# A gated mix of two linear-attention blocks: the second block's x^T phi(k) in seven half-size products, and the query sums of the output stage in quarters

## The chip, the cores and the metric

The kernel runs on one core of one Trainium2 chip. The metric is device time in microseconds (us), less is better. TensorE (PE in the profile) multiplies matrices, with its weight loads shown apart as PEld; VectorE is DVE, ScalarE is ACT, GpSimd is POOL, and SyncE (SP) issues DMAs. Matrix products land in PSUM, eight banks of 128 x 512 fp32; everything else lives in SBUF.

## What is computed

```python
def block(x, wqkv, wo):                  # x 2048 x 640, H = 32 heads of 20
    q, k, v = split_heads(x @ wqkv)
    phi = lambda t: where(t > 0, t + 1, exp(t)) + 1e-6
    pq, pk = phi(q), phi(k)
    kv = einsum("bhsd,bhse->bhde", pk, v)
    z = einsum("bhsd->bhd", pk)
    num = einsum("bhqd,bhde->bhqe", pq, kv)
    den = einsum("bhqd,bhd->bhq", pq, z)[..., None] + 1e-6
    return merge_heads(num / den) @ wo
g = sigmoid((x * gate_w).sum(-1, keepdims=True))
out = g * block(x, A_wqkv, A_wo) + (1 - g) * block(x, B_wqkv, B_wo)
```

All inputs and the output are bf16. Both blocks, A and B, take the same x.

## The kernel before

S = 2048 rows of x lie in 16 tiles of 128 (`xn`, rows on partitions) and transposed in 5 tiles of 128 columns (`xT`). For each block the kernel goes through these steps:

- **K pass** (`k_chunk`, L214): 16 chunks of x times Wk in PSUM; `phi` (L193) makes phi(k) of them: an exponential on ACT (L196), a clamp (L199) and a maximum (L203) on DVE. The result is `pk`.
- **Q pass** (`q_pass`, L601): ten units of x times Wq, transposed, through the same `phi`, into `pqT`. Between units stand the column sums z (`z_rows`, `z_pass`).
- **G stage** (`g_all`, L621): GT = x^T phi(k), a 640 x 640 matrix, so that V need not be formed. In between run the denominators (`rec_pass`, L432: products, then on DVE a scaling at L441 and a reciprocal at L446) and five calls of `norm_unit` (L482), each of which spreads the reciprocals with eight matmuls into two PSUM slots and multiplies a fifth of `pqT` by them. The gate is folded into these factors. In block A each slot is first copied to SBUF by ACT (L501) and multiplied on DVE at L503; in block B only the second slot is (`if jj == 1 or b == 0`), and the first is read by DVE from PSUM.
- **KVT and M**: `kvt_pass` (L392) makes Wv^T GT, of which DVE keeps the head-diagonal blocks (L409); `m_unit` (L416) multiplies by Wo. M is 640 x 640 for each block.
- **Output stage**: out = pqA M_A + pqB M_B, by seven half-size products instead of eight (Strassen's scheme in Winograd's form). `Pair` i makes output tiles i and i + 8; p1 to p7 are its products of five matmuls each, `out_add` (L518) the sums on DVE. The scheme needs three row sums of the queries, `p_sums` (L458): k = 1 into `pqT[0]`, k = 2 and 4 into `xT`; a difference `p_diff` into `D3`; and sums of M, `m_sums`, into `TM`.

**G in block A and in block B.** Block A computes the fifth column tile of GT directly (`g_pass`, L273: 16 row tiles x 2 halves = 32 matmuls of 320 columns) and the other four by seven products (`g_strassen`, L315; `g_prod`, L306, is one product of 16 matmuls). That form needs four sums of x, `x_sum` (L289, kept in `SX`), and four of phi(k), `k_sum` (L299, kept in `TK`, which borrows block B's `pqT`). `SX` borrows `D3`, `M[0]` and `M[1]`. Block B computes all five column tiles directly: four `g_pass` calls and `g_last` (L356).

**What sets the order.** Each engine works through its instructions in the order in which they were issued; inside `with tc.manual_schedule()` that is the order of the code, outside it a scheduler decides. Before, `g_all(1, zsel)` (L688) stands outside. PSUM slots are given out in rotation (`ps`, L63): a matmul that starts a slot waits until DVE or ACT has read what was in it. The output stage opens its own banks after `banks.close()`.

The three sums `p_sums(slice(0, HB))` (L698) for the rows of pairs 0 to 3 come first in the output stage, and one sum each for the rows of pairs 4 to 7 after pairs 1, 2 and 3:

```python
            if i < 4:
                p_sums(slice(HB, SH), ((1,), (2,), (4,))[i - 1])
```

Of the kernel before, what the change touches and what calls it, by code (L numbers as in the profile page):

```python
# [8 lines left out]
P = 128  # L9
# [21 lines left out]
def kernel(  # L31
# [31 lines left out]
    def ps(name, slot=None):  # L63
# [17 lines left out]
    grow = persist.tile([1, D], BF16, name="grow")  # L81
    D3 = persist.tile([P, DT, SH], BF16, name="D3")
    d3_flat = D3[:].rearrange("p c s -> p (c s)")
    m_flat = [t[:].rearrange("p c d -> p (c d)") for t in M]
    hc, ic = ST // 2, 2 * P
    SX = {k: t[:, o:o + hc * ic].rearrange("p (i c) -> p i c", i=hc)
          for k, t, o in ((1, d3_flat, 0), (2, d3_flat, hc * ic), (3, m_flat[0], 0), (4, m_flat[1], 0))}
    t_flat = pqT[1][:].rearrange("p c s -> p (c s)")
    TK = {k: t_flat[:, n * hc * HF:(n + 1) * hc * HF].rearrange("p (i d) -> p i d", i=hc)
          for n, k in enumerate((1, 2, 3, 4))}  # L90
    lift = persist.tile([P, 1], FP32, name="lift")
    TM = [None] * 4
# [29 lines left out]
    nc.sync.dma_start(out=wq[0][:], in_=wq_dram[0][:, :, 0:D])  # L122
    nc.gpsimd.dma_start(out=grow[:], in_=gate_w.rearrange("(o f) -> o f", o=1))
# [97 lines left out]
    def k_first():  # L221

        pts = [ps("kA", (2 + i) % 4) for i in (0, 1)]

        def part(i, cs):
            for c in cs:
                for hf in range(2):
                    k_mm(0, i, c, pts[i], hf)

        for i in range(2):  # L230
            x_transpose(i, i, "dve", (0, 2, DT))
        for i in range(2):
            part(i, (0, 1))
        x_transpose(2, 0, "dve")
        for i in range(2):
            part(i, (2,))
        pts.append(ps("kA", 1))
        part(2, (0, 1, 2))
        x_transpose(3, 0, "act")
        for i in range(3):  # L240
            part(i, (3, 4))
            k_done(0, i, pts[i])
        k_chunk(0, 3, 0)
# [55 lines left out]
    def k_sum(k):  # L299
# [3 lines left out]
        a, b = {1: (b12, b11), 2: (b22, TK[1]), 3: (b22, b12), 4: (b21, TK[2])}[k]  # L303
        add_rows(TK[k], a, b, ALU.subtract)
# [10 lines left out]
    def g_strassen(norm):  # L315

        x11, x12 = [xn[:, k:k + hc, 0:ic] for k in (0, hc)]
        x22 = xn[:, hc:ST, ic:2 * ic]
        b11 = pk[:, 0:hc, 0:HF]
        b21, b22 = [pk[:, hc:ST, n * HF:(n + 1) * HF] for n in range(2)]  # L320
        lo, hi = slice(0, HF), slice(HF, D)

        def temp(name):
            return work.tile([P, 2, HF], FP32, tag="gt", name=name, bufs=3)

        def add(dst, pt, sb):
            nc.vector.tensor_tensor(out=dst, in0=pt[:, :, 0:HF], in1=sb[:], op=ALU.add)

        even, odd = ps("gs0", 0), ps("gs1", 1)
        g_prod(even, x11, b11, True)  # L330
        p1 = temp("p1")
        nc.scalar.copy(out=p1[:], in_=even[:, :, 0:HF])
        g_prod(odd, SX[2], TK[2], True)
        u2 = temp("u2")
        add(u2[:], odd, p1)
        k_sum(4)
        norm()
        g_prod(even, x12, b21, False)
        nc.scalar.copy(out=GT[:, 0:2, lo], in_=even[:, :, 0:HF])
        norm()  # L340
        x_sum(4)
        g_prod(odd, SX[3], TK[3], False)
        u3 = temp("u3")
        add(u3[:], odd, p1)
        norm()
        even = ps("gs0", 0)
        g_prod(even, SX[1], TK[1], True)
        add(GT[:, 2:4, hi], even, u3)
        norm()
        g_prod(odd, x22, TK[4], False)  # L350
        add(GT[:, 2:4, lo], odd, p1)
        g_prod(even, SX[4], b22, False)
        add(GT[:, 0:2, hi], even, u2)
        norm()

    def g_last(b, c, slots):  # L356

        for hf, slot in enumerate(slots):
            pt = ps(f"g{'AB'[b]}", slot)
            for i in range(ST):  # L360
                g_mm(c, i, hf, pt)
            nc.scalar.copy(out=GT[:, c, hf * HF:(hf + 1) * HF], in_=pt[:, hf, 0:HF])
# [119 lines left out]
    def norm_unit(b, parts, rts, slots):  # L482

        pts = [ps(f"ex{'AB'[b]}", s) for s in slots]
        for k, (m, h) in enumerate(parts):
            for j in range(4):
                nc.tensor.matmul(  # L487
                    pts[j // 2][:, j % 2, k * RB:(k + 1) * RB], lhsT=E4[32 * j:32 * j + 32, m * P:(m + 1) * P],
                    rhs=rts[h][32 * j:32 * j + 32, :], start=True, stop=True,
                )  # L490
        (m0, h0), (m1, h1) = parts
        for jj in range(2):
            src = pts[jj][:].rearrange("p j (k n) -> p j k n", n=RB)
            if h0 == h1:
                r0 = h0 * 2 * HB + jj * HB
                dst = pqT[b][:, m0:m1 + 1, r0:r0 + HB].rearrange("p k (j n) -> p j k n", n=RB)
            else:
                dst = pqT[b][:, m0, :].rearrange("p (k u j n) -> p u j k n", k=2, u=2, n=RB)[:, jj]
            if jj == 1 or b == 0:
                ex = work.tile([P, 2, 2, RB], BF16, tag="ex", name="ex")  # L500
                nc.scalar.copy(out=ex[:], in_=src)  # L501
                src = ex[:]
            nc.vector.tensor_tensor(out=dst, in0=src, in1=dst, op=ALU.mult)  # L503
# [17 lines left out]
    def tmp(name):  # L521
        return work.tile([P, HF], FP32, tag=name, name=name)

    class Pair:

        def __init__(self, i):
            self.i = i
            self.osb = [work.tile([P, D], BF16, tag=f"osb{k}", name=f"osb{k}", bufs=3) for k in range(2)]
# [9 lines left out]
        def p2(self):  # L538
            prod(self.at("w"), pqT[1][:, :, 0:SH], M[1][:, :, 0:HF], self.i, True)
            out_add(self.osb[0][:, 0:HF], self.at("w"), self.p1s[:])  # L540
# [4 lines left out]
        def p6(self):  # L545
            prod(self.at("x"), xT[:, :, 0:SH], TM[1], self.i, False)
            self.u2 = tmp("u2")
            nc.scalar.copy(out=self.u2[:], in_=self.at("x"))  # L548
            self.u3 = tmp("u3")
# [17 lines left out]
        def p4(self):  # L567
            prod(self.at("y"), pqT[1][:, :, SH:S], TM[3], self.i, False)
            out_add(self.osb[1][:, 0:HF], self.at("y"), self.u2[:])
            nc.sync.dma_start(out=rows_of(self.i + ST // 2), in_=self.osb[1][:])  # L570
# [24 lines left out]
    def tm_pair(tag, ks):  # L595

        t = wpool.tile([P, 2, DT, HF], BF16, tag=tag, name="TM" + tag)
        for n, k in enumerate(ks):
            TM[k] = t[:, n]

    def q_pass(b, units):  # L601
# [11 lines left out]
        for k, (m, h) in enumerate(units):  # L613
            if b == 1 and k == 3:
                turn[0] = (turn[0] + 1) % 4
            if b == 0 and k < 2:
                (k_sum, x_sum)[k](2 + k)
            q_unit(b, m, h, b == 0)
        return zsel

    def g_all(b, zsel):  # L621

        units = [((m, h), (m + 1, h)) for h in range(2) for m in (0, 2)] + [((DT - 1, 0), (DT - 1, 1))]

        def norm():
            norm_unit(b, units.pop(0), rts, (2, 3))
# [37 lines left out]
    wk[1] = load_w(1, "k", nc.sync)  # L664
    with tc.manual_schedule():
        gate_columns()
        k_chunk(0, ST - 1)
        k_sum(1)
# [14 lines left out]
        load_wo(1, nc.sync)  # L683
        zsel = q_pass(1, [(m, h) for h in range(2) for m in range(DT)])
        tm_pair("wk", (0, 3))
        add_rows(TM[0], M[0][:, :, HF:D], M[0][:, :, 0:HF], ALU.subtract)
    tm_pair("wq", (1, 2))
    g_all(1, zsel)  # L688
    def late_pool(name):
        return tc.tile_pool(name=name, bufs=1, space=bass.MemoryType.PSUM, reuse_waits="tile")  # L690

    def bank(pool, name, n=1):
        return pool.tile([P, HB] if n == 1 else [P, n, HB], FP32, tag=name, name=name)

    banks.close()
    outer = ctx.enter_context(late_pool("outer"))
    with tc.manual_schedule():
        p_sums(slice(0, HB))  # L698
        half = ST // 2
        acc = {k: [bank(outer, f"o{k}{n}") for n in range(2)] for k in "xz"}  # L700
# [79 lines left out]
```

## Time and profile before

| | us |
|---|---|
| median of three runs (198.02 to 198.65) | 198.16 |
| the profiled execution | 197.97 |
| its span, first to last instruction | 196.2 |
| PE busy | 191.6 |
| DVE busy | 148.8 |
| ACT busy | 82.3 |

A line of a view gives the engine, the line of the kernel, the operation, what it writes and reads ("out<-in"), how often, and how long. In the chain of waits each line is a start, a length and the work on the path that ended last. In the timeline it is start, length, engine, line, operation, and in brackets the idle time before it and what ended that. The 1.8 us that the profiled execution's time has over its span lie before the first and behind the last instruction; the output's DMAs end there.

### The profile page before, as it was taken

The page shows a single profiled execution, that of the slowest core. Times are in us where ns is not written, and L with a number is a line of the kernel's source. Part 1 is how long each engine was busy: PE and PEld are TensorE (multiplying, and loading weights), DVE is VectorE, ACT ScalarE, POOL GpSimd, SP SyncE. Part 2 cuts the span into 40 slices and gives each one's busy share as a digit, 9 for nine tenths or more (in the row PEclk, how much of TensorE's full clock was granted, in tenths as well). Part 3 has the DMA queues.
Part 4 walks back from the last instruction along what each step waited for, and adds up shares of the span by engine and source line. Part 5 has one row for each costly group of instructions (what it writes and reads, how often), then busy time and mean ns, then how long its engine had stood idle before and what let it go on. Part 6 is the DMA issues. An engine that isn't in the chain of part 4 may idle for free.

```text
span 196.2 us, 3675 instructions
## 1 busy us (share of the span) xinstructions
PE 191.6 (98%) x1520; PEld 122.8 (63%) x1520; DVE 148.8 (76%) x242; ACT 82.3 (42%) x110; POOL 9.2 (5%) x23
## 2 busy tenths in 40 slices
PE   8999999999999999999999999999999999999992
PEld 3656557664576666777764444576667777777771
DVE  4288868898989896888887677768779798885553
ACT  2155455555931874366652554413552520122110
POOL 7920000000000000000000000000000000000000
PEclk9999999999999999999999999999999999999999
DMA  6976569970050000320071000000000002122112
GB/s 188 306 148 72 104 161 373 252 196 6 2 167 3 0 0 3 78 89 3 0 158 36 2 0 0 0 3 0 3 0 0 3 0 100 72 82 78 72 70 69
DMA packets 18318, 14.22 MB, mean 72 GB/s; under 512 B 8782, under 2 KB 18302, under 8 KB 18302
## 3 DMA queue, kind: packets, MB, share of 16 engines
q1 hardware_dynamic: 17694, 13.34, 25.6%
q10 hardware_dynamic: 576, 0.66, 0.9%
q8 instruction: 12, 0.20, 0.4%
q14 instruction: 4, 0.03, 0.0%
q0 software_dynamic: 32, 0.00, 0.0%
HBM read 9.40 MB, written 2.62 MB: 61 GB/s over the span
## 4 chain that ended last, share of the span: by engine, by line
PE 95%; DVE 2%; ACT 1%; issue 0%; DVEq 0%; ACTq 0%
PE gB L284 11%; PE kB L206 11%; PE qB L251 11%; PE kA L206 10%; PE gs L310 8%; PE qA L251 7%; PE ox L514 6%; PE oy L514 5%; PE oz L514 5%; PE qA L262 4%; PE ow L514 2%; PE gA L284 2%; PE warm L154 2%; PE mA L427 1%; DVE osb L519 1%; PE xt L187 1%
## 5 line engine op out<-in xcount | busy, mean ns | idle before, releaser
L206 PEld LDWEIGHTS <-xT 128*128 128x128 bf16 x320 | 31.1, 99 | 13.1 <-DVE xT L191 0.4
L199 DVE TENSOR_SCALAR e<-e 128x640 bf16<-128x640 bf16 (+1 forms) x52 | 19.3, 371 | 12.4 <-ACT e L196 11.5
L284 PEld LDWEIGHTS <-xn 128*128 128x128 bf16 x192 | 18.3, 98 | 8.4 <-issue 1.3
L206 PE MATMUL kA<-wkA,xT 128*128 128x320 bf16 x160 | 23.5, 304 | 0.0
L284 PE MATMUL gB<-pk,xn 128*128 128x320 bf16 x160 | 22.9, 299 | 0.0
L206 PE MATMUL kB<-wkB,xT 128*128 128x320 bf16 x160 | 22.9, 299 | 0.0
L251 PE MATMUL qB<-xT,wqB 128*128 128x512 bf16 x100 | 22.0, 379 | 0.0
L251 PEld LDWEIGHTS <-wqB 128*128 128x128 bf16 x100 | 9.6, 98 | 11.4 <-issue 0.3
L196 ACT ACTIVATE e<-kB 128x640 bf16<-128x640 f32 x16 | 11.3, 705 | 10.7 <-PE kB L206 10.7
L196 ACT ACTIVATE e<-qB 128x1024 bf16<-128x1024 f32 x10 | 10.2, 1024 | 13.1 <-PE qB L251 13.1
L203 DVE SCALAR_TENSOR_TENSOR pk<-kA,e 128x640 bf16<-128x640 f32 x16 | 13.2, 824 | 2.0 <-PE kA L206 0.5
L196 ACT ACTIVATE e<-qA 128x1024 bf16<-128x1024 f32 x10 | 10.2, 1024 | 10.7 <-PE qA L262 5.3
L196 ACT ACTIVATE e<-kA 128x640 bf16<-128x640 f32 x16 | 11.1, 706 | 8.2 <-PE kA L206 7.5
L203 DVE SCALAR_TENSOR_TENSOR pk<-kB,e 128x640 bf16<-128x640 f32 x16 | 13.2, 824 | 1.7
L251 PE MATMUL qA<-xT,wqA 128*128 128x512 bf16 x60 | 13.6, 379 | 0.0
L203 DVE SCALAR_TENSOR_TENSOR pqTB<-qB,e 128x1024 bf16<-128x1024 f32 x10 | 12.2, 1224 | 1.4 <-DVE e L199 0.5
L548 ACT COPY u<-ox 128x320 f32<-128x320 f32 x8 | 3.4, 428 | 20.9 <-PE ox L514 20.9
L501 ACT CAST ex<-exA 128x1024 bf16<-128x1024 f32 x10 | 9.6, 1017 | 5.8 <-PE exA L487 4.9
L514 PEld LDWEIGHTS <-xT 128*128 128x128 bf16 x85 | 8.1, 98 | 2.9
L251 PEld LDWEIGHTS <-wqA 128*128 128x128 bf16 x60 | 5.7, 98 | 6.7 <-issue 0.3
L514 PEld LDWEIGHTS <-pqTA 128*128 128x128 bf16 x85 | 8.0, 98 | 2.9
L514 PEld LDWEIGHTS <-pqTB 128*128 128x128 bf16 x80 | 7.8, 98 | 3.0
(118 smaller groups left out, 272.7 us busy)
## 6 DMA issues: line engine op xcount, KB each, us to landing
out_dram<-osb SPq DMA_DIRECT2D x15, 160.0 KB, 1.8
xn<-in_A_x_dram SPq DMA_DIRECT2D x3, 640.0 KB, 6.2
wqA<-in_A_wqkv_dram SPq DMA_DIRECT2D x1, 800.0 KB, 6.0
wvA<-in_A_wqkv_dram SPq DMA_DIRECT2D x1, 800.0 KB, 10.2
wkB<-in_B_wqkv_dram SPq DMA_DIRECT2D x1, 800.0 KB, 5.2
wqB<-in_B_wqkv_dram SPq DMA_DIRECT2D x1, 800.0 KB, 4.8
wvB<-in_B_wqkv_dram SPq DMA_DIRECT2D x1, 800.0 KB, 4.7
woA<-in_A_wo_dram SPq DMA_DIRECT2D x1, 750.0 KB, 13.7
```

Source lines behind the costliest of these rows:

```text
L154: nc.tensor.matmul(warm[:, 0, :], lhsT=one_l, rhs=one_r, start=True, stop=True)
L196: nc.scalar.activation(out=e[:], in_=src, func=ACT.Exp)
L199: nc.vector.tensor_scalar(e[:], e[:], 1.0, EPS, op0=ALU.min, op1=ALU.add)
L203: nc.vector.scalar_tensor_tensor(out=dst, in0=src, scalar=1.0 + EPS, in1=e[:], op0=ALU.add, op1=ALU.max)
L206: nc.tensor.matmul(pt[:, hf, 0:HF], lhsT=xT[:, c, i * P:(i + 1) * P], rhs=wk[b][:, c, hf * HF:(hf + 1) * HF], start=(c == 0), stop=(c == D ...
L251: nc.tensor.matmul(pt[:, u, :], lhsT=wq[b][:, c, m * P:(m + 1) * P], rhs=xT[:, c, n * HB:(n + 1) * HB], start=(c == 0), stop=(c == DT - 1),)
L262: nc.tensor.matmul(pt[:, u, :], lhsT=wq[b][:, c, (m + u) * P:(m + u + 1) * P], rhs=xT[:, c, n * HB:(n + 1) * HB], start=(c == 0), stop=(c ...
L284: nc.tensor.matmul(pt[:, hf, 0:HF], lhsT=xn[:, i, c * P:(c + 1) * P], rhs=pk[:, i, hf * HF:(hf + 1) * HF], start=(i == 0), stop=(i == ST - 1),
L310: nc.tensor.matmul(pt[:, n, 0:HF], lhsT=left[:, i, n * P:(n + 1) * P], rhs=right[:, i, :], start=(first and i == 0), stop=(i == hc - 1), s ...
L501: nc.scalar.copy(out=ex[:], in_=src)
L514: nc.tensor.matmul(dst, lhsT=left[:, c, r0:r0 + P], rhs=right[:, c, :], start=(first and c == 0), stop=(c == DT - 1), skip_group_check=not ...
L548: nc.scalar.copy(out=self.u2[:], in_=self.at("x"))
```

## The change

- **Block B's GT by `g_strassen`.** `g_all` has one form for both blocks: `g_pass` for the fifth column tile, a `k_sum`, `rec_pass`, `g_strassen`. `g_last` goes. The sums of x of block A are kept: `S3` is a tensor of its own for SX 1 to 3 (before they lay in `D3` and `M[0]`), SX 4 stays in `M[1]`, which block B fills only afterwards. Block B's sums of phi(k) go into `xT` and, the first, into the slot of `wkB`; two of them are made in the Q pass or at its end, one before `rec_pass`, one in `g_strassen`. The difference `TM[0]` moves from behind the Q pass into it.
- **Order within `g_strassen`.** In block B the fifth `norm` stands ahead of the seventh product, in block A behind it.
- **`norm_unit`** copies both slots by ACT in both blocks.
- **`g_all(1, zsel)`** and what follows are inside the hand-written order.
- **`p_sums` in quarters** of 256 rows: the first quarter's three sums behind the last G sum, behind `kvt_pass` and behind the two first p2; the second quarter's three within the turn of pair 1; the third and fourth two at a time after pairs 2 to 4. The sum that was at the end of `p2` is a step of its own, `c11`, and comes later for pairs 0 and 1.
- **Room.** `grow` shares the slot of `zr`, the temporaries of `Pair` those of `ex` and `zr`, the two output halves of a pair lie in one tile that shares a slot with p1, u2 and u3 of `g_strassen`. The output stage's banks are taken in the order z, x instead of x, z.
- **At the start** the fourth transpose of x is copied out of PSUM by DVE instead of ACT.

```diff
-        x_transpose(3, 0, "act")
+        x_transpose(3, 0, "dve")
...
-        g_prod(odd, SX[2], TK[2], True)
+        g_prod(odd, SX[2], TK[b][2], True)
         u2 = temp("u2")
         add(u2[:], odd, p1)
-        k_sum(4)
+        k_sum(b, 4)
         norm()
         g_prod(even, x12, b21, False)
         nc.scalar.copy(out=GT[:, 0:2, lo], in_=even[:, :, 0:HF])
         norm()
-        x_sum(4)
-        g_prod(odd, SX[3], TK[3], False)
+        if b == 0:
+            x_sum(4)
+        g_prod(odd, SX[3], TK[b][3], False)
...
-        g_prod(odd, x22, TK[4], False)
+        g_prod(odd, x22, TK[b][4], False)
         add(GT[:, 2:4, lo], odd, p1)
+        if b == 1:
+            norm()
         g_prod(even, SX[4], b22, False)
         add(GT[:, 0:2, hi], even, u2)
-        norm()
+        if b == 0:
+            norm()
...
-            if jj == 1 or b == 0:
-                ex = work.tile([P, 2, 2, RB], BF16, tag="ex", name="ex")
-                nc.scalar.copy(out=ex[:], in_=src)
-                src = ex[:]
-            nc.vector.tensor_tensor(out=dst, in0=src, in1=dst, op=ALU.mult)
+            ex = work.tile([P, 2, 2, RB], BF16, tag="ex", name="ex")
+            nc.scalar.copy(out=ex[:], in_=src)
+            nc.vector.tensor_tensor(out=dst, in0=ex[:], in1=dst, op=ALU.mult)
...
             q_unit(b, m, h, b == 0)
+            if b == 1 and k == 1:
+                k_sum(1, 1)
+            if b == 1 and k == 4:
+                add_rows(TM[0][:], M[0][:, :, HF:D], M[0][:, :, 0:HF], ALU.subtract)
+        if b == 1:
+            k_sum(1, 2)
         return zsel
...
-        if b == 0:
-            g_pass(b, DT - 1, 1)
-            k_sum(3)
-            rts = rec_pass(b, zsel, 2)
-            g_strassen(norm)
-            assert not units
-            return
-        g_pass(b, 0, 1)
+        g_pass(b, DT - 1, 1)
+        k_sum(b, 3)
         rts = rec_pass(b, zsel, 2)
-        g_pass(b, 1, 0)
-        for c in range(2, DT):
-            norm()
-            if b == 1 and c == DT - 1:
-                g_last(b, c, (1, 0))
-            else:
-                g_pass(b, c, (c + 1) % 2, norm if c < DT - 1 else None)
+        g_strassen(b, lambda: norm_unit(b, units.pop(0), rts, (2, 3)))
...
-        p_sums(slice(0, HB))
+        p_sums(part[0], (1,))
...
             pairs[0].p1()
             kvt_pass(1, bank(mid, "mid0", 2))
+            p_sums(part[0], (2,))
             pairs[1].p1()
...
         for p in pairs[0:2]:
             p.p2()
+        p_sums(part[0], (4,))
         m_sums((2, 3, 4), (3,))
         for p in pairs[0:2]:
             p.p7()
             p.p6()
             p.c22()
+            p.c11()
         pairs[0].p4()
         pairs[0].p3()
+        later = {2: (2, (1, 2)), 3: (2, (4,)), 4: (3, (2, 4))}
         for i in range(1, half):
...
             if after is not None:
                 after.p1()
-            if i + 2 < half:
-                after.p2()
-            elif after is None:
-                p.p2()
+            if i == 1:
+                p_sums(part[1], (1,))
+            q = after if i + 2 < half else p if after is None else None
+            if q is not None:
+                q.p2()
+                q.c11()
+            if i == 1:
+                p_sums(part[1], (2,))
             p.p4()
             p.p3(after is None)
-            if i < 4:
-                p_sums(slice(HB, SH), ((1,), (2,), (4,))[i - 1])
+            if i == 1:
+                p_sums(part[1], (4,))
+            if i in later:
+                p_sums(part[later[i][0]], later[i][1])
+            if i == 3:
+                p_sums(part[3], (1,))
```

More of the change, by code (lines that the diff above doesn't have):

```diff
@@ L80, with flat @@
     gwr = persist.tile([P, DT, H], BF16, name="gwr")
-    grow = persist.tile([1, D], BF16, name="grow")
     D3 = persist.tile([P, DT, SH], BF16, name="D3")
-    d3_flat = D3[:].rearrange("p c s -> p (c s)")
-    m_flat = [t[:].rearrange("p c d -> p (c d)") for t in M]
     hc, ic = ST // 2, 2 * P
[L86 to L90, printed above, removed]
+    def flat(t, pattern, inner, at=0):
+        n = hc * inner
+        return t[:].rearrange(pattern)[:, at * n:(at + 1) * n].rearrange("p (i n) -> p i n", i=hc)
+    S3 = persist.tile([P, 3, hc, ic], BF16, name="S3")
+    SX = {k: S3[:, k - 1] for k in (1, 2, 3)}
+    SX[4] = flat(M[1], "p c d -> p (c d)", ic)
+    TK = [{k: flat(pqT[1], "p c s -> p (c s)", HF, k - 1) for k in (1, 2, 3, 4)},
+          {k: flat(xT, "p c s -> p (c s)", HF, k - 2) for k in (2, 3, 4)}]
     lift = persist.tile([P, 1], FP32, name="lift")
-    TM = [None] * 4
+    TM = [persist.tile([P, DT, HF], BF16, name="TM0")] + [None] * 3
     ge = [persist.tile([P, 2 * RB], FP32, name=f"ge{b}") for b in "AB"]
@@ L122 @@
     nc.sync.dma_start(out=wq[0][:], in_=wq_dram[0][:, :, 0:D])
+    grow = work.tile([1, D], BF16, tag="zr", name="grow")
     nc.gpsimd.dma_start(out=grow[:], in_=gate_w.rearrange("(o f) -> o f", o=1))
@@ L297, in x_sum, with k_sum @@
         add_rows(SX[k], a, b, op)
-    def k_sum(k):
+    def k_sum(b, k):
         b11, b12 = [pk[:, 0:hc, n * HF:(n + 1) * HF] for n in range(2)]
         b21, b22 = [pk[:, hc:ST, n * HF:(n + 1) * HF] for n in range(2)]
-        a, b = {1: (b12, b11), 2: (b22, TK[1]), 3: (b22, b12), 4: (b21, TK[2])}[k]
-        add_rows(TK[k], a, b, ALU.subtract)
+        t = TK[b]
+        left, right = {1: lambda: (b12, b11), 2: lambda: (b22, t[1]), 3: lambda: (b22, b12), 4: lambda: (b21, t[2])}[k]()
+        add_rows(t[k], left, right, ALU.subtract)
     def g_prod(pt, left, right, first):
@@ L313, in g_prod, with g_strassen @@
                 )
-    def g_strassen(norm):
+    def g_strassen(b, norm):
         x11, x12 = [xn[:, k:k + hc, 0:ic] for k in (0, hc)]
@@ L323, in temp @@
         def temp(name):
-            return work.tile([P, 2, HF], FP32, tag="gt", name=name, bufs=3)
+            return work.tile([P, 2, HF], FP32, tag="osb", name=name, bufs=3)
         def add(dst, pt, sb):
@@ L346, in g_strassen @@
         even = ps("gs0", 0)
-        g_prod(even, SX[1], TK[1], True)
+        g_prod(even, SX[1], TK[b][1], True)
         add(GT[:, 2:4, hi], even, u3)
         norm()
-        g_prod(odd, x22, TK[4], False)
+        g_prod(odd, x22, TK[b][4], False)
         add(GT[:, 2:4, lo], odd, p1)
+        if b == 1:
+            norm()
         g_prod(even, SX[4], b22, False)
         add(GT[:, 0:2, hi], even, u2)
-        norm()
[L356 to L362, printed above, removed]
+        if b == 0:
+            norm()
     def z_rows(b):
@@ L519, in out_add, with tmp @@
         nc.vector.tensor_tensor(out=dst, in0=acc, in1=sb, op=ALU.add)
-    def tmp(name):
-        return work.tile([P, HF], FP32, tag=name, name=name)
+    def tmp(name, tag):
+        return work.tile([P, HF], FP32, tag=tag, name=name)
     class Pair:
@@ L527, in __init__ @@
             self.i = i
-            self.osb = [work.tile([P, D], BF16, tag=f"osb{k}", name=f"osb{k}", bufs=3) for k in range(2)]
+            t = work.tile([P, 2, D], BF16, tag="osb", name="osb", bufs=3)
+            self.osb = [t[:, k] for k in range(2)]
         def at(self, bank):
@@ L539, in p2, with c11 @@
             prod(self.at("w"), pqT[1][:, :, 0:SH], M[1][:, :, 0:HF], self.i, True)
+        def c11(self):
             out_add(self.osb[0][:, 0:HF], self.at("w"), self.p1s[:])
@@ L546, in p6 @@
             prod(self.at("x"), xT[:, :, 0:SH], TM[1], self.i, False)
-            self.u2 = tmp("u2")
+            self.u2 = tmp("u2", "ex")
             nc.scalar.copy(out=self.u2[:], in_=self.at("x"))
-            self.u3 = tmp("u3")
+            self.u3 = tmp("u3", "zr")
             out_add(self.u3[:], self.at("y"), self.u2[:])
@@ L569, in p4 @@
             out_add(self.osb[1][:, 0:HF], self.at("y"), self.u2[:])
-            nc.sync.dma_start(out=rows_of(self.i + ST // 2), in_=self.osb[1][:])
+            nc.sync.dma_start(out=rows_of(self.i + ST // 2), in_=self.osb[1])
         def p3(self, last=False):
@@ L593, in load_wo @@
         eng.dma_start(out=wo_sb[b][:, NJ - 1, :], in_=wo_dram[b][D - P:D, :])
[L595 to L599, printed above, removed]
     def q_pass(b, units):
@@ L616, in q_pass @@
             if b == 0 and k < 2:
-                (k_sum, x_sum)[k](2 + k)
+                if k:
+                    x_sum(3)
+                else:
+                    k_sum(0, 2)
             q_unit(b, m, h, b == 0)
+            if b == 1 and k == 1:
[4 more added lines that the diff above has]
+            k_sum(1, 2)
         return zsel
@@ L623, in g_all @@
         units = [((m, h), (m + 1, h)) for h in range(2) for m in (0, 2)] + [((DT - 1, 0), (DT - 1, 1))]
-        def norm():
-            norm_unit(b, units.pop(0), rts, (2, 3))
-        if b == 0:
-            g_pass(b, DT - 1, 1)
-            k_sum(3)
-            rts = rec_pass(b, zsel, 2)
-            g_strassen(norm)
-            assert not units
-            return
-        g_pass(b, 0, 1)
-        rts = rec_pass(b, zsel, 2)
-        g_pass(b, 1, 0)
-        for c in range(2, DT):
-            norm()
-            if b == 1 and c == DT - 1:
-                g_last(b, c, (1, 0))
-            else:
-                g_pass(b, c, (c + 1) % 2, norm if c < DT - 1 else None)
+        g_pass(b, DT - 1, 1)
+        k_sum(b, 3)
+        rts = rec_pass(b, zsel, 2)
+        g_strassen(b, lambda: norm_unit(b, units.pop(0), rts, (2, 3)))
         assert not units
@@ L664, with late_pool, bank @@
     wk[1] = load_w(1, "k", nc.sync)
+    def late_pool(name):
+        return tc.tile_pool(name=name, bufs=1, space=bass.MemoryType.PSUM, reuse_waits="tile")
+    def bank(pool, name, n=1):
+        return pool.tile([P, HB] if n == 1 else [P, n, HB], FP32, tag=name, name=name)
     with tc.manual_schedule():
@@ L667 @@
         k_chunk(0, ST - 1)
-        k_sum(1)
+        k_sum(0, 1)
         zsel = q_pass(0, [(m, 1) for m in range(DT)])
@@ L683 @@
         load_wo(1, nc.sync)
+        t1 = wpool.tile([P, hc, HF], BF16, tag="wk", name="T1")
+        TK[1][1] = t1[:]
         zsel = q_pass(1, [(m, h) for h in range(2) for m in range(DT)])
[L685 to L697, printed above, removed]
-        p_sums(slice(0, HB))
+        g_all(1, zsel)
+        banks.close()
+        outer = ctx.enter_context(late_pool("outer"))
+        TM[3] = wpool.tile([P, DT, HF], BF16, tag="wk", name="TM3")
+        t = wpool.tile([P, 2, DT, HF], BF16, tag="wq", name="TM12")
+        TM[1], TM[2] = t[:, 0], t[:, 1]
+        part = [slice(n * RB, (n + 1) * RB) for n in range(4)]
+        p_sums(part[0], (1,))
         half = ST // 2
-        acc = {k: [bank(outer, f"o{k}{n}") for n in range(2)] for k in "xz"}
+        acc = {k: [bank(outer, f"o{k}{n}") for n in range(2)] for k in "zx"}
         pairs = [Pair(i) for i in range(half)]
```

## The prediction

> **What bounds the kernel now.** I read the page's busy times and slices first, then the chain of waits in order of time, then the groups by shape for prices, then the timeline around each place that the change touches.
>
> ```profile
> PE 191.6 (98%) x1520; PEld 122.8 (63%) x1520; DVE 148.8 (76%) x242; ACT 82.3 (42%) x110; POOL 9.2 (5%) x23
> ...
> PE   8999999999999999999999999999999999999992
> ...
> DVE  4288868898989896888887677768779798885553
> ...
> PE 95%; DVE 2%; ACT 1%; issue 0%; DVEq 0%; ACTq 0%
> ```
>
> PE is busy in every slice from the second to the last but one, and 95% of the chain is PE. So matmul time that goes is time saved, as long as the DVE sums that replace it come before PE asks for them. DVE has room on average (76%), but the slices say 8 and 9 where the change adds to it. The chain, by place:
>
> ```profile
> 11.37 0.83 DVE pk L203
> ...
> 12.24 4.48 PE qA L262 x20
> ...
> 53.13 4.35 PE gA L284 x32
> ...
> 75.82 0.33 PE exA L487 x8
> 76.15 2.82 PE kB L206 x20
> ...
> 125.19 4.35 PE gB L284 x32
> ...
> 150.42 0.68 PE ox L514 x5
> 151.10 1.43 PE mid L401 x30
> ```
>
> From 12.24 to 189.9 every line but the final ones is PE. Block A's G stage, in the form that B is to get, runs from 53.13 to 76.15: 23.02 us. Block B's runs from 125.19 to 150.42: 25.23 us. Both hold the same denominators and five norms.
>
> **Part 1, the products: -2.1.** B has 5 x 32 = 160 matmuls of 320 columns, the new form 32 + 7 x 16 = 144. Sixteen at 4.35/32 = 0.136 us are 2.18; the two stages as measured differ by 25.23 - 23.02 = 2.21. A's stage ends with a norm, whose 0.1 us of refill stands in the next block (20 matmuls take 2.82 there and 2.72 elsewhere); B's ends with a product, so I take -2.11. All its matmuls have rows in A with the same 299 to 300 ns each, whatever they read.
>
> **Part 2, the sums of phi(k) on DVE: 0 on the path.** Four of 1.48 us each are added.
>
> ```profile
> L451 DVE TENSOR_TENSOR D<-pqTA 128x1280 bf16<-128x1280 bf16 x4 | 3.3, 815 | 0.0
> ...
> L451 DVE TENSOR_TENSOR pqTB<-pk 128x2560 bf16<-128x2560 bf16 x2 | 3.0, 1483 | 0.0
> ```
>
> Consecutive DVE instructions start about 0.08 us before the last one's printed end, so a sum takes 1.40 of queue. In B's Q pass PE needs 2.16 us for a unit and DVE 1.67 (0.43 + 1.22 and gaps), 0.40 idle as the timeline prints it. The first sum comes behind unit 5 (its DVE work over at 117.2) and makes unit 6's clamp start at 118.6 instead of 117.65. Unit 6 is over at 120.2; PE starts unit 9, in the same PSUM slot, at 120.9: 0.6 to spare. Unit 7 starts late, unit 8 on time; `TM[0]` (0.98) behind unit 8 is made up by unit 10, which DVE has done at 128.0, as now. The second and third sum fill 128.0 to 130.8, where DVE does `TM[0]` and then waits 1.86 for the denominators. These end on PE at 130.75, and DVE takes them at 130.85, as in A to 0.1 us. The fourth stands where A's does. A's 1.22 us `x_sum` before the fourth product has no counterpart in B, so B's DVE is ahead of A's from there. A's stage shows one PE wait of 0.06 us, which is in its 23.02. If this cover were gone, see the first rival.
>
> **Part 3, the last norm and the last sum of G: +0.5.** In B the order is: fifth norm on PE (call its start N), seventh product, then p1 of pair 0, then `kvt_pass`. On DVE the last sum GT stands behind both multiplications of that norm. A's last norm gives their times:
>
> ```profile
> 76.18 1.93 ACT L501 CAST ex<-exA 128x1024 bf16<-128x1024 f32 x2 [2.66 <-PE exA L487]
> 77.23 0.69 DVE L503 TENSOR_TENSOR pqTA<-ex,pqTA 128x1024 bf16<-128x1024 bf16 x1 [0.55 <-ACT ex L501]
> ```
>
> Casts from N + 0.36 to N + 2.29, second multiplication to N + 2.94, the sum (0.82) to N + 3.76. PE has done norm (0.33), product (2.28) and p1 (0.68) at N + 3.29. `kvt_pass` waits for that sum with its first matmul (it also takes over its PSUM slot), so PE waits 0.5. Before, it waited for no one: the last copy was over 0.2 us earlier. Bounds: 0.2 (if the sum could start at the product's end) and 0.9 (if DVE is 0.4 late). Behind the waiting sum on DVE stand a quarter `p_sums` (0.82) and the KVT masks; `kvt_pass` lasts 1.43, so the quarter is done when the masks are due.
>
> The two casts cost DVE nothing: 687 ns instead of 1224 ns for the first slot, five times. ACT gets five more casts of 1.02 in a stage where it is busy 9 of 25 us. The Trainium skill ("VectorE: DVE Perf Modes", "Rules for kernel authors") would have an elementwise step on a matmul's output either read PSUM directly or copy it first if many steps follow; here one follows, so by that rule the copy is wrong. This case's rows agree for the chain of one norm: in B now the direct multiplication starts at 135.56 and the second one ends at N + 2.36, against N + 2.94. By the rule kept for the last norm, the wait would be 0.2 and the total 0.3 lower.
>
> **Part 4, quarters in the output stage: +0.1.** A quarter costs 815 ns (the row of D above, the same shape), a half 1.48; so 0.15 more for each half. The first two quarters fall in places where DVE is idle: 0.81 before the first TM sum, and the wait for `kvt_pass`. The third takes the place of the two c11 sums, which move behind c22. That puts DVE 0.4 us later when pair 0's last sums come, and the second quarter's k = 1 and 2 go before pair 1's. The timeline there:
>
> ```profile
> 163.21 0.48 DVE L519 TENSOR_TENSOR osb<-oz,u 128x320 bf16<-128x320 f32 x1
> 164.21 0.49 DVE L519 TENSOR_TENSOR osb<-ow,p1s 128x320 bf16<-128x320 f32 x1 [0.52 <-PE ow L514]
> ...
> 165.98 0.84 PE L514 MATMUL ox<-TMwq,xT 128*128 128x320 bf16 x5
> ```
>
> In these times: pair 0's last sum ends its queue at 164.0, quarter k = 1 at 164.8, c11 of pair 2 at 165.2, quarter k = 2 at 166.1. PE's p6 of pair 2 reads that sum and would start at 165.98: a wait of 0.1. The following uses have 0.7 or more to spare (p3 of pair 2 at 169.4 needs k = 4, ready at 167.6). Pair 3's first sum needs the landing of pair 0's outputs: issued by 164.6, 1.8 to land, wanted at 168.9. Bounds: 0 and 0.6 (each 0.1 that DVE is later is 0.1 more). The last pair's chain behind PE does not change.
>
> **Part 5, the start: -0.1.** The fourth transpose's copy leaves ACT (692 ns) for DVE (492). The chain goes from that copy over ACT's exponential and DVE's clamp (0.82 there, 0.34 elsewhere, while POOL still works) to PE's 0.20 us wait at 12.24. The exponential's own input is ready at 9.63, so at most 0.15 of ACT comes forward, and the clamp may still be held by POOL until about 11. Bounds 0 and -0.2. SP's and POOL's lists of instructions keep their order; `grow` in the slot of `zr` makes block B's z wait for a DMA of the first 5 us.
>
> **Sum.** -2.11 + 0.5 + 0.1 - 0.1 = -1.6. Against the profiled execution's 197.97 that is 196.4; the median of the runs, 198.16, stands 0.19 above it, which would give 196.55. I say **196.5**.
>
> **Rivals.**
> *DVE becomes the bound in B's G stage and at pair 2.* Without any overlap of consecutive instructions (1.75 for a unit, 1.48 for a sum), DVE takes the denominators at 131.5 instead of 130.85. Then PE waits 0.2 at the third norm, 0.7 at `kvt_pass`, 0.6 at p6 of pair 2: -2.11 + 1.5 and no gain at the start, 197.4. For it: the 9s of the DVE line. Against: A's stage, with one DVE sum more, has a wait of 0.06. Chance 0.20.
> *PE waits nowhere*, because casts and sums land sooner than A's last norm shows: -2.21 and -0.2, 195.6. For it: PE has no wait above 0.2 in the whole trace. Against: the count in part 3. Chance 0.15.
> *Slower: a quarter costs DVE what a half does,* 1.48, if a sum of five short rows in place is bound by something else than its elements. Then pair 2 waits 0.1 + 3 x 0.67 = 2.1, and DVE has 5 x 0.49 + 2 x 1.48 = 5.4 us for each of the three next pairs of 4.76 on PE, 1.9 more: 198.16 - 1.6 + 3.9 = 200.5. It decides from about 1.1 us a quarter on. For it: DVE is busy 80% of that stage now. Against: the row of D, same shape, 815 ns. Chance 0.05.
> The forecast has 0.60.
>
> **Chances and range.** A measurement of this kernel can tell about 0.3%, 0.6 us. Faster by more: the forecast, the second rival and half of the first, 0.85; within: the other half, 0.10; slower: 0.05. The range for 8 in 10 goes from the second rival to the first, with 0.1 and 0.2 for the spread of the runs (198.02 and 198.65 around 198.16): 195.5 to 197.6.
>
> **What would show it.** G stage of B in the chain of 23.0 to 23.3 us instead of 25.23; a PE wait of some 0.5 at L401 for DVE's last GT; one of about 0.1 at the first `ox<-TM12,xT` of pair 2; no PE wait in B's Q pass; quarter sums at 0.8 us; the output stage as long as now to 0.2. I am wrong if PE waits for `k_sum` or a norm in B, or if the output stage grows by more than 0.6.

## The result, and the profile after

The changed kernel takes 196.62 us (median of six runs, 196.04 to 196.98), the kernel before 198.13 on the same chip: a ratio of 0.9914, 95% interval 0.9892 to 0.9936. Measured twice more beside the kernel before, on chip 9, it gave 0.9934 (0.9908 to 0.9960) and 0.9934 (0.9909 to 0.9960). The forecast was 196.5, within 195.5 to 197.6.

The page's first and second parts of the changed kernel's profile:

```profile
PE 188.6 (97%) x1497; PEld 120.8 (62%) x1504; DVE 155.4 (80%) x258; ACT 84.9 (44%) x111; POOL 9.2 (5%) x23
...
PE   8999999999999999999999999999998999999992
...
DVE  4388869888989796888786689999787899888553
```

PE has 3.0 us less to do (a few of its records are missing), DVE 6.6 more, and there is one new 8 in PE's line. The chain in order of time, at the places shown of before:

```profile
11.88 0.22 PE qA L265
...
16.20 5.43 PE kA L209 x40
...
124.66 4.35 PE gB L287 x32
...
145.16 0.38 PE exB L487 x8
145.55 0.07 ACT ex L500
145.62 0.82 issue
146.44 1.03 ACT ex L500
147.46 0.02 issue
147.49 0.69 DVE pqTB L501
148.18 0.74 DVE GT L331
148.92 0.04 issue
148.96 1.59 PE mid L401 x30
150.56 0.69 PE ox L512 x5
...
164.16 0.72 PE ox L512 x5
...
187.99 0.03 ACTq L549
```

The eight lines from 145.16 are part 3 of the prediction: the fifth norm, its second cast, its second multiplication, the last sum of G, and only then `kvt_pass`. By stage, as differences of such starts; the two of the profile before that were not shown yet are

```profile
16.72 5.43 PE kA L206 x40
...
189.93 0.03 ACTq L548
```

| stage | before | after | difference |
|---|---|---|---|
| fifth K chunk of A to B's G stage | 16.72 to 125.19 | 16.20 to 124.66 | -0.01 |
| B's G stage to `kvt_pass` | 125.19 to 151.10 | 124.66 to 148.96 | -1.61 |
| `kvt_pass` to the end of PE's last product | 151.10 to 189.93 | 148.96 to 187.99 | +0.20 |
| the three together | 173.21 | 171.79 | -1.42 |

Ahead of the first stage another 0.52 lies between the two profiles. The changed kernel itself reaches that stage at 15.93, 16.20 and 16.74 in its three profiles, so this is not the change's; the experiments on the start say more. PE's waits, longest first:

```profile
PE warm L157 <- PEq L768: 0.8, 1, 0.8
PE mid L401 <- DVE GT L331: 0.5, 1, 0.5
PE xt L190 <- DMA xn<-in_A_x_dram: 0.4, 1, 0.4
```

The first is at the very start and stands in the profile before too. The second is the only one that the change added to PE's matmuls. None names a `k_sum` or a norm.

### The profile page after: what moved, and what is told of

Its sections match the earlier page's. It is cut to its first block, busy times and chain, and to the rows that moved or that the text cites. A ratio compares the mean times of both kernels' runs of the same rounds, so it can differ in the third digit from the quotient of the medians.

```text
span 194.3 us, 3665 instructions
## 1 busy us (share of the span) xinstructions
PE 188.6 (97%) x1497; PEld 120.8 (62%) x1504; DVE 155.4 (80%) x258; ACT 84.9 (44%) x111; POOL 9.2 (5%) x23
## 4 chain that ended last, share of the span: by engine, by line
PE 91%; DMA 2%; DVE 2%; issue 1%; ACT 1%; ACTq 0%; DVEq 0%
PE gs L314 15%; PE kB L209 11%; PE qB L254 11%; PE kA L209 11%; PE qA L254 7%; PE ox L512 5%; PE oy L512 5%; PE oz L512 5%; PE qA L265 4%; DMA xn<-in_A_x_dram 2%; PE ow L512 2%; PE gB L287 2%; PE gA L287 2%; PE mA L427 1%; DVE osb L517 1%; PE exB L487 1%
## 5 line engine op out<-in xcount | busy, mean ns | idle before, releaser
L202 DVE TENSOR_SCALAR e<-e 128x640 bf16<-128x640 bf16 (+1 forms) x52 | 18.8, 361 | 9.3 <-ACT e L199 8.3
L209 PE MATMUL kA<-wkA,xT 128*128 128x320 bf16 x160 | 23.0, 299 | 0.0
L206 DVE SCALAR_TENSOR_TENSOR pqTB<-qB,e 128x1024 bf16<-128x1024 f32 x10 | 12.2, 1224 | 1.0
L314 PEld LDWEIGHTS <-xn 128*128 128x128 bf16 x96 | 8.9, 98 | 4.5 <-issue 1.3
L314 PEld LDWEIGHTS <-S 128*128 128x128 bf16 x96 | 9.1, 98 | 4.2 <-issue 0.8
L500 ACT CAST ex<-exB 128x1024 bf16<-128x1024 f32 x10 | 9.6, 1017 | 3.7 <-PE exB L487 3.7
```

The costliest lines, as they stand in the source:

```text
L202: nc.vector.tensor_scalar(e[:], e[:], 1.0, EPS, op0=ALU.min, op1=ALU.add)
L206: nc.vector.scalar_tensor_tensor(out=dst, in0=src, scalar=1.0 + EPS, in1=e[:], op0=ALU.add, op1=ALU.max)
L209: nc.tensor.matmul(pt[:, hf, 0:HF], lhsT=xT[:, c, i * P:(i + 1) * P], rhs=wk[b][:, c, hf * HF:(hf + 1) * HF], start=(c == 0), stop=(c == D ...
L314: nc.tensor.matmul(pt[:, n, 0:HF], lhsT=left[:, i, n * P:(n + 1) * P], rhs=right[:, i, :], start=(first and i == 0), stop=(i == hc - 1), s ...
```

## The experiments

All kernels ran beside the kernel before on their chip, in three series: e1 to e4 (chip 11); the second measurement of the changed kernel, e5, e7 and e8 (chip 9); the third one, e10, e11 and e12 (chip 9). Executions of one kernel differ by 1 to 2 us; as far as the profiles show, they differ at the start, where x lands at different times, and in e3 by the clock as well. So beside the time I give **the PE stretch**: from the fifth K chunk of block A (`kA x40` in the chain) to the end of PE's last product (`ACTq` behind it). It is 171.79 to 171.80 in the three profiles of the changed kernel.

| kernel | median us | ratio, interval | PE stretch |
|---|---|---|---|
| before (first profile) | 198.13 | 1 | 173.21 |
| changed (first) | 196.62 | 0.9914, 0.9892 to 0.9936 | 171.79 |
| changed (second) | 196.71 | 0.9934, 0.9908 to 0.9960 | 171.80 |
| changed (third) | 196.46 | 0.9934, 0.9909 to 0.9960 | 171.80 |
| e1 p1 of pair 1 as cover | 196.61 | 0.9941, 0.9919 to 0.9963 | 171.70 |
| e2 first slot read from PSUM | 197.13 | 0.9979, 0.9963 to 0.9996 | 172.44 |
| e3 query sums in halves | 199.37 | 1.0086, 1.0061 to 1.0111 | 176.02 |
| e4 quarters alone | 197.52 | 0.9998, 0.9982 to 1.0015 | 173.26 |
| e5 copy on ACT | 197.32 | 0.9970, 0.9946 to 0.9993 | 171.80 |
| e7 one sum twice | 197.89 | 0.9998, 0.9976 to 1.0020 | 172.98 |
| e8 three sums left out | 196.79 | 0.9934, 0.9909 to 0.9959 | 171.80 |
| e10 cover, product split | 196.67 | 0.9935, 0.9909 to 0.9961 | 171.43 |
| e11 copy alone, on before | 197.60 | 0.9998, 0.9979 to 1.0017 | 173.21 |
| e12 copy on ACT, again | 196.95 | 0.9949, 0.9926 to 0.9972 | 171.80 |

The kernel before had medians of 197.50 to 198.13 in the series; compare ratios, not medians. The ratios are those on record and not quotients of the medians shown.

**Are the quarters what makes it pay? (e3, e4)** The first puts the query sums of the changed kernel back into halves, the second puts quarters into the kernel before.

```diff
-        p_sums(part[0], (1,))
+        p_sums(slice(0, HB))
...
+            if i < 4:
+                p_sums(slice(HB, SH), ((1,), (2,), (4,))[i - 1])
```

> The changed kernel with the query sums in halves, where they were before the change: all three for the rows of pairs 0 to 3 ahead of the output stage, the others one each behind pairs 1 to 3. Theory (the quarters are what lets the seven products pay): DVE does 3 x 1.40 us behind the last sum of G, so the masks of KVT start at about 153.0 instead of 150.6 in the changed kernel's times, PE waits 2.1 us for them at the first M unit, and the time is 198.5 to 198.9, no better than before the change. Rival (DVE has room, the quarters only cost): 196.4 to 196.6.

> The kernel before the change with the query sums in quarters and c11 as a step of its own, and nothing else of the change; block B's G stays at 160 matmuls. Theory: the quarters save and cost nothing by themselves, since the three halves lie beside the last product of G there; PE waits at most 0.1 us at the sixth product of pair 2: 198.0 to 198.3. Rival (the quarters are part of the gain): below 197.7.

Both theories held in kind. Alone, the quarters are worth nothing: 0.9998, and a stretch of 173.26 against 173.21. With halves in the old places, the seven products make the kernel slower than it was, by more than I had worked out. In e3, PE's longest wait, what DVE does ahead of it, then a table of stretches (length, busy time of PE, its weight loads, DVE, ACT and POOL, then the granted clock, the DMA share and GB/s):

```profile
PE mid L427 <- DVE KVT L409: 2.4, 1, 2.4
```

```profile
148.80 1.48 DVE L451 TENSOR_TENSOR pqTA<-pqTA,pqTB 128x2560 bf16<-128x2560 bf16 x1
...
150.32 1.49 DVE L451 TENSOR_TENSOR xT<-pqTA 128x2560 bf16<-128x2560 bf16 x1
...
151.84 1.49 DVE L451 TENSOR_TENSOR xT<-pqTB,xT 128x2560 bf16<-128x2560 bf16 x1
153.25 1.14 DVE L409 TENSOR_TENSOR KVT<-mid,maskE 120x120 bf16<-120x120 f32 x6
```

```profile
151.00:153.60 2.60, 0.23 (x3) 0.02 (x1) 2.57 (x4) 0.42 (x1) 0.00 (x0) 1.00 0.00 0
153.60:155.00 1.40, 1.40 (x10) 0.98 (x11) 0.79 (x5) 0.61 (x1) 0.00 (x0) 0.97 0.00 0
155.00:158.00 3.00, 3.00 (x13) 1.66 (x11) 1.77 (x6) 1.47 (x3) 0.00 (x0) 0.50 0.00 0
158.00:159.00 1.00, 1.00 (x8) 0.67 (x6) 0.00 (x0) 0.21 (x1) 0.00 (x0) 0.83 0.00 0
```

PE waits 2.4 us for the masks, behind three halves in DVE's queue, as expected to 0.3: the second and the third half read what the one before wrote, and each starts 1.52 after it instead of the 1.40 that I had taken. Then, 1.3 us after PE is busy again, its granted clock is 0.50 from 154.9 to 158.3 by the table: 3.4 us at half the clock, so the wait is paid a second time, with 1.7 us. These two are nearly all of the stretch's 4.2 us more. The halved clock does not come each time. Two of the six executions, 200.28 and 200.56 (the profiled one), have a mean granted clock of 0.991; the other four, 199.08 to 199.50, have 0.999 to 1.000. Even these four are slower than every execution of the kernel before in the series (197.17 to 198.49). What e3 does not separate is size from place: it puts whole halves, and all three of them, ahead of the masks. As an estimate, one half there (1.5 instead of 0.82 behind the last sum of G, which ends at 148.92) would still end at about 150.4, before the masks start at 150.6; so spreading the sums may matter more than their size, and no run tells.

**What does the wait for the last sum of G cost? (e1, e10)** Nothing is added; products that PE does anyway move in front of the wait.

```diff
             pairs[0].p1()
+            pairs[1].p1()
             kvt_pass(1, bank(mid, "mid0", 2))
             p_sums(part[0], (2,))
-            pairs[1].p1()
+            pairs[0].p5()
             for c in range(3):
                 m_unit(1, c, "act", bank(mid, f"mid{(c + 1) % 2}", 2))
-                if c == 0:
-                    pairs[0].p5()
+                if c == 1:
+                    pairs[1].p5()
                 if c < 2:
                     m_sums((c,))
-            pairs[1].p5()
```

> The changed kernel with the first product of pair 1 moved ahead of kvt_pass, the fifth product of pair 0 put between kvt_pass and the first M unit, and that of pair 1 behind the second M unit. Nothing is added or taken away. Theory (the 0.51 us that PE waits for the last sum of G, and the 0.16 us longer first stretch behind that wait, are the whole loss there): the wait falls to 0.1 or less, the M units from the second on come 0.4 to 0.6 us sooner, and the time is 0.3 to 0.6 us below the changed kernel's 196.6, so 196.0 to 196.3. Rival (the wait only hides others, DVE's masks and the copies of M, which then end last): within 0.2 us of 196.6.

The wait is gone, and the stretch is only 0.10 shorter: the rival was right here. In e1 the chain goes from the third M unit over its copy on ACT (0.70) to the last of M's five tiles, whose PSUM bank that copy sets free; PE waits 0.24 there and starts again slowly (0.71 for four matmuls, elsewhere 0.55). The first two M units, whose masks DVE is still making, take 1.27 instead of 1.09. Together that is 0.58 of the 0.67 that was won. e10 cuts pair 1's fifth product, two matmuls before the third M unit (c = 2 in the code) and three between the tiles c = 3 and c = 4:

> The first experiment's order, with the fifth product of pair 1 cut in two: two of its matmuls between the second and the third M unit, three between the third and fourth tile of M. In the first experiment the wait for the last sum of G was gone, but PE then waited 0.24 us, and 0.16 for the refill, for the copy of the third M unit. Theory (those were all that stood in its way): no PE wait above 0.1 us between B's last product of G and the output stage, and 0.4 to 0.6 us below the changed kernel of the same call. Rival (DVE's copies and sums of M end last whatever PE does): within 0.2 us of it.

Now the list of PE's waits has only the one at the very start, and the stretch is 171.43, 0.37 shorter than the changed kernel's. The other 0.3 of the 0.67 stands where PE is counted as busy: 1.27 instead of 1.09 again, and 0.66 instead of 0.55 for the tile c = 3. The time does not show the gain: 196.67 against 196.46 of the changed kernel beside it, ratios 0.9935 and 0.9934. So the theory is right on the waits, not on the 0.4 to 0.6 us, and no version here is shown to be faster than the changed kernel.

**Were the two casts free? (e2)** Block B's first slot goes straight from PSUM to DVE again.

```diff
-            ex = work.tile([P, 2, 2, RB], BF16, tag="ex", name="ex")
-            nc.scalar.copy(out=ex[:], in_=src)
-            nc.vector.tensor_tensor(out=dst, in0=ex[:], in1=dst, op=ALU.mult)
+            if jj == 1 or b == 0:
+                ex = work.tile([P, 2, 2, RB], BF16, tag="ex", name="ex")
+                nc.scalar.copy(out=ex[:], in_=src)
+                src = ex[:]
+            nc.vector.tensor_tensor(out=dst, in0=src, in1=dst, op=ALU.mult)
```

> The changed kernel with block B's first slot of each norm read by DVE straight from PSUM again, as before the change. Theory: DVE's second multiplication of the last norm ends at N + 2.36 instead of N + 2.94 (N is that norm's start on PE), the last sum of G starts as soon as its product is done, PE's wait at kvt_pass falls from 0.51 to about 0.2 us, and the time from 196.6 to about 196.3. Rival (DVE is the engine that is late in B's G stage, and 0.54 us more for each of the five multiplications makes PE wait at a norm): 196.8 or more, with a PE wait in front of a norm.

Both waits came as described; in time the rival was right (197.13). PE's waits, and what DVE did ahead of the first of them:

```profile
PE exB L487 <- DVE pqTB L503: 0.9, 1, 0.9
PE warm L157 <- PEq L770: 0.8, 1, 0.8
PE mid L401 <- DVE GT L331: 0.2, 1, 0.2
```

```profile
135.24 1.48 DVE L451 TENSOR_TENSOR xT<-pk,xT 128x2560 bf16<-128x2560 bf16 x1
136.64 1.22 DVE L503 TENSOR_TENSOR pqTB<-exB,pqTB 128x1024 bf16<-128x1024 f32 x1
...
137.91 0.40 PE L487 MATMUL exB<-rT,E 32*128 32x256 bf16 x8 [0.91 <-DVE pqTB L503]
```

The wait at `kvt_pass` is 0.2 as worked out, but the second norm waits 0.9: its PSUM slot is read only when DVE has done the fourth `k_sum`. The stretch is 0.65 longer. In the changed kernel ACT reads both slots, while DVE makes the same sum:

```profile
135.08 1.93 ACT L500 CAST ex<-exB 128x1024 bf16<-128x1024 f32 x2 [1.86 <-PE exB L487]
```

It is done at 137.01, and the second norm starts at 137.27 without a wait. The kernel before, which read the first slot directly too, had no such wait and no `k_sum` there. So part of the copy's worth is that it takes the slot out of DVE's queue. How large a part, e2 does not separate: as an estimate, with 0.69 instead of 1.22 for the multiplication, 0.4 of the 0.9 would be left.

**Do the sums of phi(k) cost? (e7, e8)** e7 makes the first one twice, in place; e8 leaves out the second to fourth, of which the diff shows one.

```diff
                 k_sum(1, 1)
+                k_sum(1, 1)
```

```diff
-        k_sum(b, 3)
+        if b == 0:
+            k_sum(b, 3)
```

> The changed kernel with block B's first sum of phi(k) made twice, one right behind the other, in the Q pass: 1.40 us more of DVE's queue, nothing else. Theory (DVE has 0.6 us to spare there until PE wants the PSUM slot of unit 9): PE waits 0.8 us in front of a unit of B's Q pass, and the stretch behind is 0.16 longer: 0.8 to 1.0 us slower than the changed kernel of the same call. Rival (DVE, busy 80% of the span, takes another sum anywhere in that pass): within 0.2 us.

> The changed kernel without three of block B's four sums of phi(k), the second, third and fourth (4.2 us of DVE's queue); the products read what lies in xT instead, so block B's result is left out of the computation rightly done. Theory (those sums lie wholly beside other work): within 0.2 us of the changed kernel of the same call. Rival (DVE is what B's G stage waits for): 0.4 us faster or more.

Without the three sums the stretch is 171.80, the same to 0.01, and the time 0.9934 of before: they cost nothing. One more in the Q pass costs 1.18 us of the stretch, and the gain is gone (0.9998 of before). The sum made twice, and the wait behind it:

```profile
117.72 3.01 DVE L451 TENSOR_TENSOR T<-pk 128x2560 bf16<-128x2560 bf16 x2
...
120.64 0.42 DVE L202 TENSOR_SCALAR e<-e 128x1024 bf16<-128x1024 bf16 x1
...
122.45 1.89 PE L254 MATMUL qB<-xT,wqB 128*128 128x512 bf16 x8 [1.02 <-DVE pqTB L206]
```

The wait is 1.02, where 0.8 was expected, and 0.16 is the slow start behind it. The two sums hold the queue for 120.64 - 117.72 = 2.92, the one of the changed kernel for 1.40 (116.63 to 118.03); so the second added 1.52, and DVE's margin at that unit was 1.52 - 1.02 = 0.5 us, near the 0.6 of the prediction: room for this sum and not for two.

**Is the start part of the gain? (a0, a1, e5, e11, e12)** The second series had the changed kernel and one with the copy on ACT:

```diff
-        x_transpose(3, 0, "dve")
+        x_transpose(3, 0, "act")
```

> The changed kernel itself, on one chip with the three next ones, as what they are set against. Both theories: 0.990 to 0.994 of the kernel before, since the chip of the first experiments had the kernel before at 197.5 instead of 198.1 us.

> The changed kernel with the fourth transpose's copy on ACT again. Theory (the engine of the copy moves nothing: what makes PE wait at the start is whether DVE's first clamp begins before POOL's last pieces of E4, and that hangs on when x lands): within 0.2 us of the changed kernel of the same call, with a first clamp of 0.33 or of 0.7 to 0.8 us, as it comes. Rival (the prediction's: the copy on DVE is what took the 0.20 us wait away): 0.15 to 0.4 us slower than the changed kernel.

The profiles are alike to 0.01 us from 16.74 on, and both have a first clamp that ends at 11.26; but the medians were 0.6 apart, 197.32 and 196.71. So the third series repeated both and added the copy alone on the kernel before:

> The kernel before the change with the fourth transpose's copy on DVE, and nothing else of the change. Theory (the copy's engine is worth nothing by itself): within 0.2 us of the kernel before of the same call. Rival (the copy is part of the gain, as the 0.6 us between the two kernels of the second call hints): 0.3 to 0.7 us below it.

> The changed kernel once more, to set the next one and the two above against it: 0.991 to 0.994 of the kernel before.

> The changed kernel with the copy on ACT, once more, since the second call left a difference of 0.6 us that its profile does not show. Theory (copy without effect): within 0.2 us of the changed kernel of this call. Rival (the copy on ACT costs): 0.3 to 0.7 us above it, with the difference in the start, ahead of the fifth K chunk.

Alone the copy is worth nothing by the ratio (0.9998; the means are equal, 197.73, though the medians are 0.34 apart). On the changed kernel the medians are 0.5 apart again, 196.95 and 196.46 (the means 0.50 and 0.28 in the two series), with intervals that overlap in both. By the medians, the theory of e5 and e12, within 0.2 us, failed, and e12's rival was met. What the start shows is DVE's first clamp beside POOL's mask work, in e12 (copy on ACT), the changed kernel's first profile and e4 (copy on ACT):

```profile
10.38 0.89 DVE L202 TENSOR_SCALAR e<-e 128x640 bf16<-128x640 bf16 x1 [2.69 <-ACT e L199]
```

```profile
10.21 0.33 DVE L202 TENSOR_SCALAR e<-e 128x640 bf16<-128x640 bf16 x1 [0.79 <-ACT e L199]
```

```profile
10.24 0.33 DVE L199 TENSOR_SCALAR e<-e 128x640 bf16<-128x640 bf16 x1 [2.69 <-ACT e L196]
```

The 14 profiles agree on this. POOL's last two pieces start at about 9.6 and 10.3 (10.34 in the profile before) and take 0.71 to 0.72 when nothing meets them. A clamp that begins in the last 0.1 us of the first of them or between the two, at 10.18 to 10.29, takes 0.33 (five profiles, one of them with the copy on ACT), as does the one that begins at 11.30, after POOL's work. A clamp that begins at another time while a piece runs takes 0.51 to 0.89 and ends 0.17 to 0.19 us after that piece (eight profiles); in e12 PE then waits 0.26. The copy's engine moves the clamp very little: it begins 1.59 to 1.60 after the fourth transpose starts with the copy on DVE (ten profiles), 1.64 to 1.65 with ACT (four). So the copy is worth 0.05 us at that place, and more only if these 0.05 carry the clamp into a piece. When x lands, by contrast, differs by more than 1 us: in e7 PE's transposes wait for it until 7.67, in the third profile of the changed kernel until 6.21. The 0.5 us between the medians may then be chance in the landing; that stays open, since no profile shows where it would be and the copy alone on the kernel before does not have it.

## Why the prediction was right, point by point

- **Products, -2.11.** In e1 the start of p1 of pair 0 stands in the chain:

```profile
125.16 4.35 PE gB L287 x32
...
148.28 1.36 PE ox L512 x10
```

The G stage up to it takes 23.12 us, against 25.23: -2.11.
- **Sums of phi(k), 0.** Right: no PE wait names one, and three of them left out change nothing (e8). Their margin in the Q pass was 0.5, near the 0.6 (e7).
- **Last sum of G, +0.5.** PE's wait was 0.51. What the sum lacked is the slow start behind a wait: the stretch of `kvt_pass` to the next product is 1.60 instead of 1.43. So this term was 0.67, mis-sized by 0.16. The same 0.16 stands behind the 1.02 wait of e7, and in the profile before behind the 0.20 wait at 12.24 (20 matmuls in 4.48, elsewhere 4.32). The 0.16 and the 0.04 of the next point are the +0.20 in the table by stage.
- **Quarters, +0.1.** The first p6 of pair 2 came 0.04 late (0.72 instead of 0.68). The quarters took 0.81 to 0.82. That sums left in halves at the old places would cost more than the change wins (e3), the prediction did not say.
- **Start, -0.1.** Not shown. The copy moves the clamp by 0.05, and e11's ratio (0.9998, 0.9979 to 1.0017) is too wide to tell 0.1 us. The difference of the two profiles there, 0.52, is 0.16 from when x landed (the fourth transpose starts at 8.78 and 8.62) and 0.36 from the clamp beside POOL.
- **The copy in the norms.** The prediction's figure for the direct read in the last norm alone, a wait of 0.2, came as said (e2), and with 0.3 less wait there "the total 0.3 lower" may hold; no run has the direct read in the last norm only. In all five norms it cost 0.65. What the prediction left out is who waits for the PSUM slot: it priced the copy by DVE's time (687 instead of 1224 ns) alone. The Trainium skill's rule on elementwise steps ("VectorE: DVE Perf Modes", "Rules for kernel authors") speaks of an engine's throughput; e2 shows that here the release of the slot counts too, with a wait of 0.91.

Without the start the forecast comes to -1.51 and the stretch changed by -1.42: 0.16 too little for the wait, 0.06 too much for the quarters. The median came within 0.12 us of the forecast; the six executions spread over 0.94, so a hit that close is luck, while the terms behind it are shown one by one. The first rival (DVE as the bound) did not come; e7 shows that it was one further sum in the Q pass away. The second rival (PE waits nowhere) did not come either, by the 0.51 at `kvt_pass`; its argument that PE had no wait above 0.2 before overlooks the 0.8 at the very start, which changes nothing here. The rival "slower" was wrong in its mechanism, since a quarter costs 0.82; but e3 shows that the same engine at another place, the masks behind whole halves, would have made the change slower.

## What to carry to other kernels

Where PE is the bound, price a change by the matmuls that it takes out, then go through the in-order queue of the engine that gets the replacement work and ask, at each place, what PE wants next from behind it; average busy shares (80% here) say nothing on that. Cut such work into pieces that fit the gaps, and spread them, before moving more of it there. A copy out of PSUM that looks like extra work can be what frees the slot in time.

## What the runs showed of the hardware that was not expected

- A PE wait cost 0.16 us more than its length, in the first stretch behind it, at waits of 0.20, 0.24, 0.51 and 1.02 us. Behind the 0.91 of e2 it was 0.07 (a norm of eight small matmuls, 0.40 instead of 0.33), behind the 2.4 of e3 0.22.
- A wait of 2.4 us, in a stretch in which PE was busy 0.23 of 2.60 us, was followed by a granted clock of 0.50 for 3.4 us, in e3's profile and, by the mean clock of 0.991, in one more of its six executions; in the other four, with 0.999 to 1.000, it was not. The Trainium skill ("TensorE: Matmul & The Clock Gate", "Why this matters for your kernels") warns of idle gaps above about 3 us; here a shorter one sufficed at times, and the wait of 1.02 in e7's profile left the mean clock at 1.000.
- DVE's clamp of 128 x 640 bf16 in SBUF took 0.33 us, or 0.51 to 0.89 when it began while a piece of POOL's work on the mask `E` ran, and then ended 0.17 to 0.19 after that piece. Where it began first, POOL's next piece took 0.75 to 0.87 instead of 0.72. A copy of the same size out of PSUM took 0.49 amid the same work. The Trainium skill ("GPSIMD Engine Reference", "Specifications") names contention of VectorE's two-port modes with GpSimd for SBUF; these rows agree with it, if the clamp runs in such a mode, which no trace shows.
